# Batch 0's first attention in another order: q loaded ahead of v, and q's and a1's transposes ahead of the products with v

## The chip, the cores and the metric

The kernel runs on one core of one Trainium2 chip. The metric is the time of one execution on the device in microseconds (us). Three runs of the kernel before gave 770.55, 770.76 and 771.34 us; the median is 770.76 us.

## The reference

```python
def sm_attn(qq, kk, vv):                      # softmax attention, scale = 1/8
    s = scale * np.matmul(qq, kk.transpose(0, 1, 3, 2))
    s = s - np.max(s, axis=-1, keepdims=True)
    a = np.exp(s)
    a = a / (np.sum(a, axis=-1, keepdims=True) + 1e-09)
    return np.matmul(a, vv)
p_packed = sm_attn(p, k, v)                   # 32 packed rows attend to 576 keys
out = sm_attn(q, p_packed, p_packed)          # 576 queries attend to the 32 packed rows
...
h = x @ w_in                                  # x: (8*576, 512) from out; w_in (512, 2048)
g = np.maximum(h, 0.0) + np.log1p(np.exp(-np.abs(h)))
return (g @ w_out).astype(np.float32)         # w_out (2048, 512)
```

There are 8 batches of 8 heads, 576 rows of 64 numbers each, and 32 packed rows per head. The weights `w_in` and `w_out` arrive as 64-bit floats; everything else is 32 bits wide.

## The kernel before

**Per batch.** The heads of a batch are worked on in two groups of four (`g` = 0, 1). For each group the first attention takes these steps: k is turned by TensorE (`transposed`, tiles `psT_k`, copied by ScalarE into `T_k`); the scores of p against k (`scores1`, `ps1`) are copied to `a1`; maximum and exponential are taken (`softmax1_*`); the weights are turned (`a1_transposed`, tile `psa`, copied to `a1T`) and multiplied by v (`packed_products`, tile `psp`). VectorE scales the result (`pp`), TensorE turns it (`psx`), VectorE copies it (`pt`): `pt` is p_packed with its columns turned. For the second attention q is turned like k (`psT_q`, `T_q`), multiplied by `pt` (`scores2`, tile `ps2`), and VectorE transposes the scores into `a2` (L354), takes the softmax over packs of 32 (L362 to L374, with the exponential on ScalarE at L366) and transposes it into `aT` (L378).

**The feed-forward part.** It never forms p_packed times weights: `make_m` multiplies `pt` by `w_in` (tile `psm`) and splits it into a high and a low half (`mh`, `ml`), `weights` splits `aT` into `at_h` and `at_l`, and `gemm1` multiplies them into `ph`. A *unit* is one batch `b` and one slice `f` of 128 of the 2048 inner columns, so there are 16 units in a batch. Each unit has 12 products for `ph` (L606), the softplus on ScalarE and VectorE (`softplus`, tile `e`, L626 to L631), a split into `gh` and `gl`, and, two units later, 12 products with `w_out` into `acc` (L642). The next batch's attention is spread over the units of the batch ahead of it.

**The conversion of the weights.** `convert` brings 64-bit weights to 32 bits, in 32 items that are numbered in the order of use (item 0 and 1: `w_in`, 2 and 3: `w_out`, 4 and 5: `w_in`, and so on). Each item is loaded by SyncE (`x_i`, `x_o`, or a place in `rest`), read twice by ScalarE (`m` at L200, `r` at L204), worked on twice by VectorE (`t` at L206 and L211) and added by GpSimd (L219). A `w_out` item also has a ScalarE cast (`wo_h`, L238) and a VectorE subtraction (`wo_l`, L244). The buffers of `m`, `r`, `t` and `x` are few, so an item waits for an earlier one to be used up. All items are spread over batch 0: over its attention first, then over its units.

**What sets the order.** TensorE's order is that of the code. For the other engines a scheduler orders the instructions by its own estimates and by a priority, which is raised for batch 0's attention. Once ordered, each engine works its row strictly from front to back. SyncE's queue starts p, k (two groups), items 0 and 1, v (two groups), q (two groups), then items 2 to 5. A load waits until the load eight places ahead of it has landed; q's two loads in the profile wait for k's two. Batch 0's q lies in the columns of `w_in_sb` that are filled last.

**PSUM.** During batch 0's attention six banks go round. After it `make_m` and the turns of batch 1's k share two banks, so `psm` of the second slice waits for ScalarE's copies of `T_k`.

Of the kernel before, what the change touches and what calls it, by code (L numbers as in the profile page):

```python
# [9 lines left out]
F32 = mybir.dt.float32  # L10
# [16 lines left out]
def pack_attention_then_softplus_ffn(  # L27
# [11 lines left out]
    B, H, S, D = q.shape  # L39
    J = p.shape[2]  # L40
    DM, DFF = w_in.shape
    P = 128
    NP = 96
    SI = S // NP
    HS = SI // 2
    C = S // 2
    G = H * J // P
    HG = H // G
# [12 lines left out]
    work = ctx.enter_context(tc.tile_pool(name="work", bufs=2))  # L61
# [25 lines left out]
    def bank(nm):  # L87
        if spare:
            spare.append(spare.pop(0))
            pool, tag = spare[-1]  # L90
            return pool.tile([P, 512], F32, tag=tag, name=nm)
        return ps_m.tile([P, 512], F32, tag="m", name=nm)
# [165 lines left out]
    def transposed(nm, b, g, hh):  # L258

        src = loaded[nm, b, g]  # L260
        ps = bank(f"psT_{nm}_{b}_{g}_{hh}")
        for i in range(HS):
            nc.tensor.transpose(
                ps[:, i * NP:(i + 1) * NP],
                src[:, hh, 2 * i:2 * i + 2, :].rearrange("x s d -> x (s d)"),
                ident[:NP, :NP],
            )
        dst = work.tile([P, C], F32, tag="T", name=f"T_{nm}_{b}_{g}_{hh}", bufs=4)
        nc.scalar.copy(dst, ps[:, :C])  # L269
        return dst  # L270
# [12 lines left out]
    def products1(b, g, c, kT, ps=None):  # L283
        cols = slice(b % BG * J, (b % BG + 1) * J)
        return scores(1, b, g, c, lambda hh: pT[:, g * HG + hh, cols], kT, ps)

    def scores1(b, g, c, kT, a1):
        nc.scalar.copy(a1[:, c * C:(c + 1) * C], products1(b, g, c, kT))

    def softmax1_max(b, g, a1):  # L290
        m = small.tile([P, 1], F32, tag="m1", name=f"m1_{b}_{g}", bufs=1)
        nc.vector.reduce_max(m, a1, axis=AX.X)
        nm = small.tile([P, 1], F32, tag="nm1", name=f"nm1_{b}_{g}")
        nc.vector.tensor_scalar_mul(nm, m, -scale)
        return nm

    def softmax1_exp(b, g, a1, nm):
        z = small.tile([P, 1], F32, tag="z1", name=f"z1_{b}_{g}")
        nc.scalar.activation(a1, a1, AF.Exp, bias=nm, scale=scale, accum_out=z)
        return z  # L300

    def softmax1_sum(b, g, z):
        rs = small.tile([P, 1], F32, tag="rs", name=f"rs_{b}_{g}")
        nc.vector.tensor_scalar_add(rs, z, 1e-9)
        nc.vector.reciprocal(rs, rs)
        return rs

    def a1_transposed(b, g, c, a1, a1T):
        ps = bank(f"psa_{b}_{g}_{c}")
        for i in range(HS):  # L310
            o = c * C + i * NP
            nc.tensor.transpose(ps[:NP, i * P:(i + 1) * P], a1[:, o:o + NP], ident)  # L312
        nc.scalar.copy(
            a1T[:, c * HS:(c + 1) * HS, :].rearrange("x s j -> x (s j)"), ps[:NP, :HS * P]
        )
# [17 lines left out]
    def packed(b, g, a1T, rs):  # L333
        ps = bank(f"psp_{b}_{g}")[:, :D]
        packed_products(b, g, a1T, ps)
        return packed_scaled(b, g, ps, rs)

    def packed_transposed(b, g, pp):
        ps = bank(f"psx_{b}_{g}")
        nc.tensor.transpose(ps[:, :P], pp.rearrange("x i d -> x (i d)"), ident)  # L340
        pt = small.tile([P, P], F32, tag="pt", name=f"pt_{b}_{g}", bufs=2 * G)
        nc.vector.tensor_copy(pt, ps[:, :P])
        return pt
# [7 lines left out]
    def scores2(b, g, qT):  # L351
        a2 = work.tile([P, S], F32, tag="a2", name=f"a2_{b}_{g}", bufs=2)
        for c in range(2):
            nc.vector.transpose(a2[:, c * C:(c + 1) * C], products2(b, g, c, qT))  # L354
        return a2

    def by_pack(a2):
        return a2.rearrange("x (n j) -> x n j", j=J)

    def softmax2_exp(b, g, a2):  # L360
        m = small.tile([P, S // J, 1], F32, tag="m2", name=f"m2_{b}_{g}")
        nc.vector.reduce_max(m.rearrange("x n o -> x (n o)"), by_pack(a2), axis=AX.X)  # L362
        nc.vector.tensor_tensor(
            by_pack(a2), by_pack(a2), m.broadcast_to([P, S // J, J]), op=ALU.subtract
        )
        nc.scalar.activation(a2, a2, AF.Exp, scale=scale)  # L366

    def softmax2_div(b, g, a2):
        z = small.tile([P, S // J, 1], F32, tag="z2", name=f"z2_{b}_{g}")
        zf = z.rearrange("x n o -> x (n o)")  # L370
        nc.vector.reduce_sum(zf, by_pack(a2), axis=AX.X)
        nc.vector.tensor_scalar_add(zf, zf, 1e-9)
        nc.vector.reciprocal(zf, zf)
        nc.vector.tensor_tensor(  # L374
            by_pack(a2), by_pack(a2), z.broadcast_to([P, S // J, J]), op=ALU.mult
        )
        aT = work.tile([P, S], F32, tag="aT", name=f"aT_{b}_{g}", bufs=G)
        nc.vector.transpose(aT, a2)  # L378
        res[b]["aT"][g] = aT

    def attention_first(b):
# [71 lines left out]
        softmax2_div(b, 1, a2)  # L453
        yield

    def attention_next(b):


        a1 = [work.tile([P, S], F32, tag="a1", name=f"a1_{b}_{g}") for g in range(G)]
        if b == FIRST:  # L460
            for nm in ("k", "v"):
                for g in range(G):
                    load(nm, b, g)
                    yield
            yield
        kT = [quads("k", b, 0)]
        yield
        yield
        for c in range(2):
            scores1(b, 0, c, kT[0], a1[0])  # L470
        yield
        nm = softmax1_max(b, 0, a1[0])
        kT.append(quads("k", b, 1))
        yield
        load("q", b, 0)
        z = softmax1_exp(b, 0, a1[0], nm)
        yield
        rs = softmax1_sum(b, 0, z)
        yield
        a1T = work.tile([NP, SI, P], F32, tag="a1T", name=f"a1T_{b}_0", bufs=1)  # L480
        for c in range(2):
            a1_transposed(b, 0, c, a1[0], a1T)
            yield
        yield
        ps = [bank(f"ps1_{b}_{c}") for c in range(2)]
        packed_products(b, 0, a1T, ps[0][:, C:C + D])
        s1 = [products1(b, 1, c, kT[1], ps[c]) for c in range(2)]
        for c in range(2):
            nc.scalar.copy(a1[1][:, c * C:(c + 1) * C], s1[c])
        pp = packed_scaled(b, 0, ps[0][:, C:C + D], rs)  # L490
        yield
        load("q", b, 1)
        load("k", b + 1, 0)
        nm = softmax1_max(b, 1, a1[1])
        qT = [quads("q", b, 0)]
        yield
        z = softmax1_exp(b, 1, a1[1], nm)
        res[b]["pt"].append(packed_transposed(b, 0, pp))
        yield
        rs = softmax1_sum(b, 1, z)  # L500
        yield
        a1T = work.tile([NP, SI, P], F32, tag="a1T", name=f"a1T_{b}_1", bufs=1)
        for c in range(2):
            a1_transposed(b, 1, c, a1[1], a1T)
            yield
        load("k", b + 1, 1)
        qT.append(quads("q", b, 1))
        yield
        ps = [bank(f"ps2_{b}_{c}") for c in range(2)]
        packed_products(b, 1, a1T, ps[0][:, C:C + D])  # L510
        s2 = [products2(b, 0, c, qT[0], ps[c]) for c in range(2)]
        pp = packed_scaled(b, 1, ps[0][:, C:C + D], rs)
        a2 = work.tile([P, S], F32, tag="a2", name=f"a2_{b}_0", bufs=2)
        for c in range(2):
            nc.vector.transpose(a2[:, c * C:(c + 1) * C], s2[c])
        yield
        yield
        load("v", b + 1, 0)
        res[b]["pt"].append(packed_transposed(b, 1, pp))
        yield  # L520
        softmax2_exp(b, 0, a2)
        yield
        yield
        softmax2_div(b, 0, a2)
        yield
        a2 = scores2(b, 1, qT[1])
        yield
        softmax2_exp(b, 1, a2)
        yield
        load("v", b + 1, 1)  # L530
        yield
        softmax2_div(b, 1, a2)
        yield

    def attention(b):
        return attention_first(b) if b < FIRST else attention_next(b)
# [169 lines left out]
    pt = load_pack(0, (nc.sync, nc.scalar))  # L706
# [1 line left out]
    for g in range(G):  # L708
        load("k", 0, g)
    next(conv)  # L710
    for nm in ("v", "q"):
        for g in range(G):
            load(nm, 0, g)
    next(conv)
    res = [{"pt": [], "aT": {}, "m": {}} for _ in range(B)]
# [1 line left out]
    spare += [(ps_acc, "acc")] * NT + [(ps_m, "m")] * 2  # L717
    pack_transposed(0, pt)
    due = 0.0
    steps = attention(0)  # L720
    for st in range(NF * NT):
        with tc.high_priority(offset=FRONT):
            if next(steps, steps) is steps:
# [17 lines left out]
    for u in range(len(units) + LAG):  # L741
        if u < len(units):
            b, f = units[u]
# [7 lines left out]
            if f == NF - 1:  # L751
                if (b + 2) % BG == 0 and b + 2 < B:
                    pt = load_pack((b + 2) // BG, (nc.sync,))
# [33 lines left out]
        if u + 2 < len(units):  # L787


            nb, c = units[u + 2][0], units[u + 2][1] * P  # L790
# [31 lines left out]
```

## Time and profile before

| | us |
|---|---|
| median of three runs (lowest, highest) | 770.76 (770.55, 771.34) |
| the profiled execution, whole | 770.49 |
| its span, from the first to the last instruction | 768.7 |
| busy in it: TensorE matmul | 731.6 (95%) |
| VectorE | 529.7 (69%) |
| ScalarE | 431.8 (56%) |
| GpSimd | 98.7 (13%) |
| loads and stores | 55.97 MB, mean 73 GB/s |

The profile gives times in us from the first instruction. A row of the timeline is: start, time taken, engine, line, operation, written tile and read tiles (without numbers), shapes, count, and in brackets the idle time of the engine just before with what ended it. A `q` behind an engine's name (`SPq`) is its queue's own work, such as starting a load. In a table by windows each engine has its busy time in the window, with the number of instructions in brackets. TensorE's column of the clock is the share of its full clock that was granted.

### The profile page before, as it was taken

The page shows a single profiled execution, that of the slowest core. Times are in us where ns is not written, and L with a number is a line of the kernel's source. Part 1 is how long each engine was busy: PE and PEld are TensorE (multiplying, and loading weights), DVE is VectorE, ACT ScalarE, POOL GpSimd, SP SyncE. Part 2 cuts the span into 40 slices and gives each one's busy share as a digit, 9 for nine tenths or more (in the row PEclk, how much of TensorE's full clock was granted, in tenths as well). Part 3 has the DMA queues.
Part 4 walks back from the last instruction along what each step waited for, and adds up shares of the span by engine and source line. Part 5 has one row for each costly group of instructions (what it writes and reads, how often), then busy time and mean ns, then how long its engine had stood idle before and what let it go on. Part 6 is the DMA issues. An engine that isn't in the chain of part 4 may idle for free.

```text
span 768.7 us, 14169 instructions
## 1 busy us (share of the span) xinstructions
PE 731.6 (95%) x5360; PEld 579.9 (75%) x5360; DVE 529.7 (69%) x1092; ACT 431.8 (56%) x1057; POOL 98.7 (13%) x166
## 2 busy tenths in 40 slices
PE   6657998999999999999999999999999999999997
PEld 4445776787778877877887877878787877888886
DVE  2696879975787568665877568675777558665554
ACT  5667977655555455565555355565555364565540
POOL 1143444200000000000000000000000000000110
PEclk9957999999999999999999999999999999999999
DMA  9877655534312144033312134033311220010002
GB/s 218 233 187 172 177 151 130 123 73 71 69 32 72 30 64 93 1 94 62 63 31 70 32 63 93 1 87 62 63 32 56 44 32 1 1 55 1 1 1 69
DMA packets 149668, 55.97 MB, mean 73 GB/s; under 512 B 116320, under 2 KB 142944, under 8 KB 149600
## 3 DMA queue, kind: packets, MB, share of 16 engines
q1 hardware_dynamic: 149328, 55.00, 31.9%
q8 instruction: 42, 0.69, 0.4%
q14 instruction: 26, 0.21, 0.1%
q10 hardware_dynamic: 272, 0.07, 0.0%
HBM read 45.61 MB, written 9.44 MB: 72 GB/s over the span
## 4 chain that ended last, share of the span: by engine, by line
PE 85%; ACT 5%; DVE 5%; DMA 3%; issue 1%; POOL 1%; SPq 0%; DVEq 0%; ACTq 0%; POOLq 0%
PE acc L642 42%; PE ph L606 26%; PE acc_m L642 6%; PE psm L563 4%; PE ps L277 2%; DMA w_in_sb<-in_q 2%; PE psa L312 1%; PE ps L320 1%; DMA k<-in_k 1%; ACT e L628 1%; ACT m L200 1%; DVE e L631 1%; ACT e L626 1%; ACT e L629 1%; DVE t L206 1%
## 5 line engine op out<-in xcount | busy, mean ns | idle before, releaser
L642 PE MATMUL acc<-wo_h,gh 128*128 128x512 f32 x512 | 207.6, 405 | 0.0
L631 DVE SCALAR_TENSOR_TENSOR e<-ph,e 128x288 f32<-128x288 f32 x256 | 113.5, 453 | 133.9 <-ACT e L629 131.3
L626 ACT ACTIVATE e<-ph 128x288 f32<-128x288 f32 x256 | 102.3, 403 | 176.4 <-PE ph L606 153.9
L642 PE MATMUL acc<-wo_l,gh 128*128 128x512 f32 x512 | 201.2, 393 | 0.0
L642 PE MATMUL acc<-wo_h,gl 128*128 128x512 f32 x512 | 200.8, 392 | 0.0
L606 PE MATMUL ph<-at_h,mh 128*128 128x288 f32 x512 | 158.3, 310 | 13.2 <-ACT at_h L545 6.9
L606 PE MATMUL ph<-at_l,mh 128*128 128x288 f32 x512 | 151.7, 299 | 2.5 <-DVE at_l L546 2.5
L606 PE MATMUL ph<-at_h,ml 128*128 128x288 f32 x512 | 152.5, 298 | 0.0
L606 PEld LDWEIGHTS ph<-at_h,mh 128*128 128x128 f32 x512 | 97.6, 191 | 48.9 <-DVE gl L619 15.1
L635 POOL COPY rest<-e 128x64 f32<-128x64 f32 x128 | 53.3, 416 | 574.0 <-DVE e L631 541.2
L642 PEld LDWEIGHTS acc<-wo_h,gh 128*128 128x128 f32 x512 | 96.3, 188 | 26.9 <-issue 12.3
L642 PEld LDWEIGHTS acc<-wo_h,gl 128*128 128x128 f32 x512 | 96.3, 188 | 21.2
L628 ACT ACTIVATE e<-e 128x288 f32<-128x288 f32 (+1 forms) x240 | 108.7, 456 | 3.7
L629 ACT ACTIVATE e<-e 128x288 f32<-128x288 f32 (+1 forms) x240 | 108.6, 455 | 2.7
L642 PEld LDWEIGHTS acc<-wo_l,gh 128*128 128x128 f32 x512 | 96.5, 188 | 13.1
L606 PEld LDWEIGHTS ph<-at_l,mh 128*128 128x128 f32 x512 | 97.5, 191 | 6.0 <-DVE at_l L546 3.1
L606 PEld LDWEIGHTS ph<-at_h,ml 128*128 128x128 f32 x512 | 97.8, 191 | 0.2
L619 DVE TENSOR_TENSOR gl<-e,gh 128x512 fp32r<-128x512 f32 x128 | 87.5, 683 | 6.0
L578 ACT CAST mh<-psm 128x512 fp32r<-128x512 f32 (+1 forms) x72 | 36.3, 539 | 60.9 <-PE psm L563 60.7
L618 DVE CAST gh<-e 128x512 fp32r<-128x512 f32 x128 | 55.5, 434 | 5.9
L579 DVE TENSOR_TENSOR ml<-psm,mh 128x512 fp32r<-128x512 f32 (+1 forms) x72 | 43.0, 624 | 22.0 <-ACT mh L578 21.8
L563 PE MATMUL psm<-w_in_sb,pt 64*32 64x512 f32 (+1 forms) x576 | 41.4, 564 | 8.3 <-ACT T_k L269 4.8
(84 smaller groups left out, 698.2 us busy)
## 6 DMA issues: line engine op xcount, KB each, us to landing
v<-in_v SPq DMA_DIRECT2D x16, 576.0 KB, 5.4
x_i<-in_moe_w_in SPq DMA_DIRECT2D x28, 256.0 KB, 4.4
k<-in_k SPq DMA_DIRECT2D x48, 144.0 KB, 3.2
q<-in_q SPq DMA_DIRECT2D x48, 144.0 KB, 3.4
x_o<-in_moe_w_out SPq DMA_DIRECT2D x11, 512.0 KB, 3.7
out<-o SPq DMA_DIRECT2D x18, 256.0 KB, 2.5
rest<-in_moe_w_out SPq DMA_DIRECT2D x5, 512.0 KB, 6.0
k<-in_k SPq DMA_DIRECT2D x4, 576.0 KB, 6.0
```

The source lines that it names most:

```text
L563: nc.tensor.matmul(ps[hh * J:(hh + 1) * J, :n], res["pt"][g][o:o + D, hh * J:(hh + 1) * J], w_in_sb[o:o + D, hh, c * n:(c + 1) * n], start ...
L578: nc.scalar.copy(mh[:, cols], ps[:, :n])
L579: nc.vector.tensor_tensor(ml[:, cols], ps[:, :n], mh[:, cols].bitcast(F32), op=ALU.subtract)
L606: nc.tensor.matmul(phs[c], x, y[:, g, c * C:(c + 1) * C], start=(i == 0), stop=(i == 3 * G - 1))
L618: nc.vector.tensor_copy(hi, x)
L619: nc.vector.tensor_tensor(lo, x, hi.bitcast(F32), op=ALU.subtract)
L626: nc.scalar.activation(es[c], hv[c], AF.Abs)
L628: nc.scalar.activation(x, x, AF.Exp, scale=-1.0)
L629: nc.scalar.activation(x, x, AF.Ln, bias=1.0)
L631: nc.vector.scalar_tensor_tensor(es[c], hv[c], 0.0, es[c], op0=ALU.max, op1=ALU.add)
L635: nc.gpsimd.tensor_copy(rest[:, rest_at(b, f), r:r + REST], e[:, NT * P:])
L642: nc.tensor.matmul(acc, x[:, cs], y[:, f, :], start=(first and i == 0), stop=(last and i == 2),)
```

## The change

Batch 0 gets an attention function of its own, `attention_zero`; batch 1 keeps `attention_first`. It differs from `attention_first` in this: q's four turns of group 0 stand directly behind a1's turns of group 0, a1's turns of group 1 follow, and only then come the products with v of group 0, its turn, and those of group 1. For that `a1T` of group 1 gets a place of its own, that of `at_h`, which is not in use yet. The division of the second softmax of group 0 is written behind the turns of q of group 1. SyncE starts q's loads ahead of v's. The diff's core:

```diff
+    def attention_zero(b):
+        a1 = [work.tile([P, S], F32, tag="a1", name=f"a1_{b}_{g}") for g in range(G)]
...
+        nm = softmax1_max(b, 1, a1[1])
+        a1T = [
+            work.tile([NP, SI, P], F32, tag=t, name=f"a1T_{b}_{g}", bufs=1)
+            for g, t in enumerate(("a1T", "at_h"))
+        ]
+        for c in range(2):
+            a1_transposed(b, 0, c, a1[0], a1T[0])
+            yield
+            if c == 0:
+                z1 = softmax1_exp(b, 1, a1[1], nm)
+        qT = []
+        for hh in range(HG):
+            qT.append(transposed("q", b, 0, hh))
+            yield
+        rs1 = softmax1_sum(b, 1, z1)
+        for c in range(2):
+            a1_transposed(b, 1, c, a1[1], a1T[1])
+            yield
+        pp = packed(b, 0, a1T[0], rs0)
+        yield
+        res[b]["pt"].append(packed_transposed(b, 0, pp))
+        yield
+        pp = packed(b, 1, a1T[1], rs1)
+        yield
+        a2 = scores2(b, 0, qT)
+        yield
+        softmax2_exp(b, 0, a2)
+        res[b]["pt"].append(packed_transposed(b, 1, pp))
...
-    for nm in ("v", "q"):
+    for nm in ("q", "v"):
         for g in range(G):
             load(nm, 0, g)
...
-    steps = attention(0)
+    steps = attention_zero(0)
```

On TensorE, between a1's turns of group 0 and the scores of q's group 0 (`psT_q`: a turn of q; `psa`: a turn of a1; `psp`: products with v; `psx`: the turn of p_packed; in the names the batch comes first, then the group), before:

```order
L263 MATMUL psT_q_0_0_0_324<-ident_82,w_in_sb_87 128x96 x3
L312 MATMUL psa_0_1_0_337<-ident_82,a1_0_1_128 96x128 x3
L312 MATMUL psa_0_1_1_342<-ident_82,a1_0_1_128 96x128 x3
L340 MATMUL psx_0_0_349<-ident_82,pp_0_0_319 128x128
L263 MATMUL psT_q_0_0_1_353<-ident_82,w_in_sb_87 128x96 x3
L320 MATMUL psp_0_1_366<-v_0_1_107,a1T_0_1_336 32x64 x24
L263 MATMUL psT_q_0_0_2_394<-ident_82,w_in_sb_87 128x96 x3
L263 MATMUL psT_q_0_0_3_401<-ident_82,w_in_sb_87 128x96 x3
L277 MATMUL ps2_0_0_0_408<-T_q_0_0_0_328,pt_0_0_351 32x288
```

The same place in the changed kernel, from the last of q's four turns on:

```order
L263 MATMUL psT_q_0_0_3_318<-ident_82,w_in_sb_87 128x96 x3
L312 MATMUL psa_0_1_0_329<-ident_82,a1_0_1_128 96x128 x3
L312 MATMUL psa_0_1_1_334<-ident_82,a1_0_1_128 96x128 x3
L320 MATMUL psp_0_0_346<-v_0_0_107,a1T_0_0_268 32x64 x24
L340 MATMUL psx_0_0_374<-ident_82,pp_0_0_371 128x128
L320 MATMUL psp_0_1_379<-v_0_1_109,a1T_0_1_269 32x64 x24
L277 MATMUL ps2_0_0_0_408<-T_q_0_0_0_296,pt_0_0_376 32x288
```

Products with v of both groups now stand between the last turn and the scores; before, those of group 0 stood in front of all these rows and three of q's turns lay around those of group 1.

On VectorE, the end of the second softmax of batch 0 (`at_l` is the last thing that the first `ph` needs; `t` and `wo_l` are the conversion's), before:

```order
L206 TENSOR_SCALAR t_4_244<-m_4_240 128x512
L373 RECIPROCAL z2_0_1_488<-z2_0_1_488 128x18
L211 SCALAR_TENSOR_TENSOR t_4_244<-m_4_240,t_4_244 128x512
L374 TENSOR_TENSOR a2_0_1_470<-a2_0_1_470,z2_0_1_488 128x576
L546 TENSOR_TENSOR at_l_0_522<-aT_0_0_448,at_h_0_521 128x576
L378 STREAM_TRANSPOSE aT_0_1_493<-a2_0_1_470 128x576
L244 TENSOR_TENSOR wo_l_89<-r_3_216,wo_h_88 128x512
L206 TENSOR_SCALAR t_5_286<-m_5_282 128x512
L546 TENSOR_TENSOR at_l_0_522<-aT_0_1_493,at_h_0_521 128x576
L211 SCALAR_TENSOR_TENSOR t_5_286<-m_5_282,t_5_286 128x512
```

And now:

```order
L211 SCALAR_TENSOR_TENSOR t_3_218<-m_3_214,t_3_218 128x512
L373 RECIPROCAL z2_0_1_488<-z2_0_1_488 128x18
L615 TENSOR_TENSOR at_l_0_522<-aT_0_0_468,at_h_0_521 128x576
L374 TENSOR_TENSOR a2_0_1_470<-a2_0_1_470,z2_0_1_488 128x576
L244 TENSOR_TENSOR wo_l_89<-r_2_189,wo_h_88 128x512
L378 STREAM_TRANSPOSE aT_0_1_493<-a2_0_1_470 128x576
L206 TENSOR_SCALAR t_4_244<-m_4_240 128x512
L244 TENSOR_TENSOR wo_l_89<-r_3_216,wo_h_88 128x512
L615 TENSOR_TENSOR at_l_0_522<-aT_0_1_493,at_h_0_521 128x576
L211 SCALAR_TENSOR_TENSOR t_4_244<-m_4_240,t_4_244 128x512
L206 TENSOR_SCALAR t_5_287<-m_5_283 128x512
L211 SCALAR_TENSOR_TENSOR t_5_287<-m_5_283,t_5_287 128x512
```

The second step of item 4 and the first of item 5 moved behind the last `at_l`. At the other end of the softmax both steps of item 2, which stood ahead of the first `a2`, moved behind it.

On ScalarE, at the first unit's softplus (`e_0_0`: batch 0, slice 0), before:

```order
L545 CAST at_h_0_521<-aT_0_0_448 128x576
L200 ACTIVATE m_6_330<-rest_90 128x512
L204 ACTIVATE r_8_458<-x_i4_246 128x512
L545 CAST at_h_0_521<-aT_0_1_493 128x576
L200 ACTIVATE m_7_359<-rest_90 128x512
L626 ACTIVATE e_0_0_541<-ph_0_0_0_527 128x288
L626 ACTIVATE e_0_0_541<-ph_0_0_1_528 128x288
```

And now:

```order
L614 CAST at_h_0_521<-aT_0_1_493 128x576
L695 ACTIVATE e_0_0_541<-ph_0_0_0_527 128x288
L200 ACTIVATE m_6_306<-rest_90 128x512
L200 ACTIVATE m_7_339<-rest_90 128x512
L204 ACTIVATE r_8_451<-x_i4_246 128x512
L695 ACTIVATE e_0_0_541<-ph_0_0_1_528 128x288
```

The first reads of items 6 and 7 moved behind the first softplus instruction, which needs `ph`.

More of the change, by code (lines that the diff above doesn't have):

```diff
@@ L454, in attention_first @@
         yield
+    def attention_zero(b):
+        a1 = [work.tile([P, S], F32, tag="a1", name=f"a1_{b}_{g}") for g in range(G)]
+        kT = []
+        for hh in range(HG):
+            kT.append(transposed("k", b, 0, hh))
+            yield
+        for c in range(2):
+            scores1(b, 0, c, kT, a1[0])
+        yield
+        nm = softmax1_max(b, 0, a1[0])
+        kT = [transposed("k", b, 1, 0)]
+        yield
+        z0 = softmax1_exp(b, 0, a1[0], nm)
+        kT.append(transposed("k", b, 1, 1))
+        yield
+        rs0 = softmax1_sum(b, 0, z0)
+        for hh in range(2, HG):
+            kT.append(transposed("k", b, 1, hh))
+            yield
+        for c in range(2):
+            scores1(b, 1, c, kT, a1[1])
+        yield
[4 more added lines that the diff above has]
+        ]
+        for c in range(2):
+            a1_transposed(b, 0, c, a1[0], a1T[0])
[3 more added lines that the diff above has]
+        qT = []
+        for hh in range(HG):
+            qT.append(transposed("q", b, 0, hh))
+            yield
+        rs1 = softmax1_sum(b, 1, z1)
+        for c in range(2):
+            a1_transposed(b, 1, c, a1[1], a1T[1])
+            yield
+        pp = packed(b, 0, a1T[0], rs0)
+        yield
+        res[b]["pt"].append(packed_transposed(b, 0, pp))
+        yield
+        pp = packed(b, 1, a1T[1], rs1)
+        yield
+        a2 = scores2(b, 0, qT)
+        yield
+        softmax2_exp(b, 0, a2)
+        res[b]["pt"].append(packed_transposed(b, 1, pp))
+        yield
+        qT = [transposed("q", b, 1, 0)]
+        yield
+        qT.append(transposed("q", b, 1, 1))
+        yield
+        qT.append(transposed("q", b, 1, 2))
+        yield
+        qT.append(transposed("q", b, 1, 3))
+        yield
+        softmax2_div(b, 0, a2)
+        a2 = scores2(b, 1, qT)
+        yield
+        softmax2_exp(b, 1, a2)
+        yield
+        softmax2_div(b, 1, a2)
+        yield
     def attention_next(b):
```

## The prediction

> **What bounds the kernel now.** I read the page first, then the chain of work that ended last in order of time, then the windows, the waits and the timeline of the first 70 us. From the page, TensorE's busy tenths and its granted clock in 40 slices of 19.2 us:
>
> ```profile
> PE   6657998999999999999999999999999999999997
> PEclk9957999999999999999999999999999999999999
> ```
>
> After the first 80 us TensorE is busy nine tenths or more. What the change touches lies in the first two slices, so the question is how much earlier or later TensorE's closed work begins. The chain there:
>
> ```profile
> 6.32 13.92 DMA w_in_sb<-in_q
> ...
> 20.38 0.71 PE psT_q L263 x3
> ...
> 53.13 1.08 PE psm L563 x8
> 54.21 3.18 PE ph L606 x12
> 57.39 0.49 PE psT_k L263 x3
> ...
> 61.12 3.25 PE ph L606 x12
> 64.36 1.28 PE acc L642 x3
> 65.64 0.93 PE ps L277 x16
> ...
> 84.32 1.79 PE ph L606 x12
> ```
>
> Batch 0's q lands at 6.32 + 13.92 = 20.24 us and TensorE, which had nothing to do, starts on it at once: the wait that the change aims at. The same 12 products take 3.2 us at 54 and 61 us and 1.8 us at 84 us. Three stretches of the windows say what limits the time after that:
>
> ```profile
> 27.80:44.50 16.70, 7.29 (x55) 5.05 (x52) 15.96 (x32) 11.98 (x23) 4.11 (x3) 0.73 0.69 179
> 53.10:66.20 13.10, 10.30 (x57) 8.04 (x57) 9.28 (x17) 9.00 (x18) 5.23 (x5) 0.50 0.95 216
> 80.00:150.00 70.00, 65.75 (x544) 48.42 (x544) 61.94 (x129) 55.83 (x117) 28.62 (x28) 1.00 0.57 145
> ```
>
> The columns are TensorE's matmuls, its weight loads, VectorE, ScalarE, GpSimd, clock. From the first scores of q to the first `ph` VectorE is busy 15.96 of 16.70 us: the second softmax and the conversion share it, and TensorE waits. From 80 to 150 us TensorE is idle for only 4.25 us, so a delay brought in there finds little to hide in.
>
> **The loads.** For v's two loads (one row, both durations) and each of q's, from issue to landing:
>
> ```profile
> L127 SPq DMA_DIRECT2D v<-in_v x2: 479/540/602, 5.0 to 5.6; - x2
> DMA to landing us min/median/max: 10.6/11.4/12.3
> ...
> L127 SPq DMA_DIRECT2D w_in_sb<-in_q x1: 1594/1594/1594, 6.3 to 6.3; - x1
> DMA to landing us min/median/max: 13.9/13.9/13.9
> ...
> L127 SPq DMA_DIRECT2D w_in_sb<-in_q x1: 666/666/666, 8.8 to 8.8; - x1
> DMA to landing us min/median/max: 15.2/15.2/15.2
> ```
>
> The four places of 576 KB land at 5.0 + 10.6 = 15.6, 17.9, 20.2 and 8.8 + 15.2 = 24.0 us. Equal bytes and equal waits swap places, so I keep the times: q's groups now land at 15.6 and 17.9 us, v's at 20.2 and 24.0. The second group of v is the one that hurts. Before, the fourth place held q's second group, which nobody needed until 28 us.
>
> **TensorE up to the scores of q.**
>
> ```profile
> 20.89 1.48 PE L312 MATMUL psa<-ident,a 128*96 128x128 f32 x6
> ...
> 23.00 1.51 PE L320 MATMUL psp<-v,a1T 96*32 96x64 f32 x48
> ...
> 25.59 2.24 PE L277 MATMUL ps<-T_q,pt 64*32 64x288 f32 x16
> 26.33 0.51 PEld L277 LDWEIGHTS ps<-T_q,pt 64*32 64x32 f32 x12 [0.56 <-ACT T_q L269]
> 28.03 2.12 PE L263 MATMUL psT_q<-ident,w_in_sb 96*128 96x96 f32 x12
> ...
> 27.83 0.48 DVE L354 STREAM_TRANSPOSE a<-ps 128x288 f32<-128x288 f32 x1 [0.65 <-PE ps L277]
> 31.90 0.48 DVE L354 STREAM_TRANSPOSE a<-ps 128x288 f32<-128x288 f32 x1 [0.71 <-PE ps L277]
> ```
>
> q's four turns (2.1 us for 12 pieces) and a1's of group 1 (1.48 us) now fall between 15.9 and 19.7 us, where TensorE was idle; they cost nothing, and the cover is the wait for v. The products of group 0 run from 20.2 to 21.7 us. Those of group 1 wait for 24.0 and end at 25.5 us, and the scores of q stand right behind them on TensorE. Before, the scores took 2.24 us, of which 0.56 went on waiting for the last copies of q, so 1.68 at most; 16 such matmuls at 65.64 us in the chain took 0.93. Between these ends VectorE's first `a2` comes at 26.5 to 27.2 us in place of 27.83: a gain of 0.6 to 1.3 us, of which I take 1.0, and not the 5 us that the freed wait suggests. From there to group 1's scores the order is unchanged (turn of p_packed, 12 turns, copies), 31.90 - 27.83 = 4.1 us, so group 1 gains the same.
>
> **VectorE up to the first `ph`.**
>
> ```profile
> 30.43 0.75 DVE L363 TENSOR_TENSOR a<-a,m 128x576 f32<-128x576 f32 x1
> ...
> L206 DVE TENSOR_SCALAR t<-m 128x512 int32<-128x512 int32 x3 | 1.2, 402 | 0.0
> ```
>
> Between the first `a2` and the last `at_l` the work on VectorE is equal: item 2's two steps came in (they were done ahead of it, in idle time), one step each of items 4 and 5 went out. But the subtraction of group 0's maximum (L363, 0.75 us) now stands behind group 1's first transposition and no longer fills the wait in front of it, so that wait grows from 0.71 to about 1.4 us. The last `at_l` gains what the start gained less 0.7: between 0 and 0.6 us, 0.3 by the value taken.
>
> **The conversion loses.** Behind the last `at_l` there is now more to do: a second step of 0.6 us and a first step of 0.35. These meet GpSimd:
>
> ```profile
> 39.43 1.64 POOL L219 TENSOR_TENSOR w_in_sb<-t,r 128x512 int32<-128x512 int32 x1 [7.11 <-DVE t L211]
> 39.88 1.82 DVE L546 TENSOR_TENSOR at_l<-aT,at_h 128x576 fp32r<-128x576 f32 x1
> 43.21 0.75 DVE L546 TENSOR_TENSOR at_l<-aT,at_h 128x576 fp32r<-128x576 f32 x1
> 44.70 1.33 POOL L219 TENSOR_TENSOR w_in_sb<-t,r 128x512 int32<-128x512 int32 x1 [3.63 <-DVE t L211]
> 44.82 1.50 DVE L206 TENSOR_SCALAR t<-m 128x512 int32<-128x512 int32 x1
> ```
>
> `at_l` takes 0.75 us alone and 1.82 beside GpSimd's addition, and `t` at L206 takes 1.50 beside it where its mean over 27.8 to 44 us is 0.40: VectorE stands still until the addition is done. Before, item 4's addition was paid in front of the last `at_l` and one step of item 5 met another. Now item 3's is paid in front of it, and items 4's and 5's, 1.3 us each, both fall behind it, on the first steps of items 5 and 7. So the conversion is late by 0.95 us of work, plus 1.2 for the added standstill, less the 0 to 0.6 gained: 1.6 to 2.1 us at items 6 to 9, 1.8 by the values taken. That items 6 and 7 are first read behind `e` of the first unit costs nothing more, since VectorE gets to them only after that.
>
> **Who waits for it.** ScalarE's copies of `T_k` stand behind reads of items 8 and 9, and `psm` of the second slice waits for them:
>
> ```profile
> PE ph L606 <- ACT at_h L545: 6.9, 2, 6.4
> PE psm L563 <- ACT T_k L269: 4.8, 2, 2.8
> ...
> 43.70 0.33 SPq L156 DMA_DIRECT2D rest<-in_moe_w_out  x1
> 52.98 0.68 ACT L204 ACTIVATE r<-rest 128x512 int32<-128x512 uint32 x1
> ```
>
> The second row holds the two waits in front of 53.13 us. Before, ScalarE read item 9 twice between its two copies of `T_k`; now the read at L204 stands ahead of both copies, where it falls in a wait, so some 0.6 of the 1.6 to 2.1 us is given back and the second copy comes 1.0 to 1.5 us late. The second unit starts as late, although the first one ended up to 0.6 us early. The load of item 10 waits for ScalarE's reads of item 7 and starts some 3 us later; in the last two rows it started 9 us ahead of its first read, so it stays hidden.
>
> **The sum.** From 54 us on I carry the delay to the end, since each engine's row goes on in nearly the same order. One thing gives back. From 61.1 to 66.2 us TensorE works without a break at half clock. If the clock returns at the same time, a start 1.0 to 1.5 us later leaves as much less at half speed, and half of it, 0.5 to 0.75 us, comes back.
>
> ```profile
> 64.00:66.00 2.00, 2.00 (x13) 1.05 (x20) 0.24 (x1) 1.54 (x3) 0.00 (x0) 0.50 0.22 88
> 66.00:68.00 2.00, 2.00 (x22) 1.19 (x7) 1.43 (x3) 0.94 (x3) 0.24 (x1) 0.94 0.00 0
> ```
>
> So the ends are +0.5 us (the second unit's smallest delay with the give-back) and +2.1 (the conversion's largest without), and I take +1.0, near TensorE's own delay, for the late units are TensorE's by the third window. The profiled execution took 770.49 us in all, 0.27 less than the median of 770.76; 770.8 + 1.0 is 771.8 us. What a measurement of this kernel tells from no change is about 0.2%, or 1.5 us, so this counts as no change.
>
> The Trainium skill, "TensorE: Matmul & The Clock Gate", Part 1, says that the clock is halved after an idle window of about 3.4 us and returns after a busy one, and that the windows run freely. This trace agrees as far as it goes: TensorE's wait of 6.4 us for `at_h` is longer than such a window, and 0.50 was granted behind it until about 66 us. By that rule the return goes by the edge of a window and not by the start of the work; a window at half speed is worth 1.7 us, so the sum by the rule would be +1.5 us, the delay without the give-back, plus or minus 1.7 (an estimate from that page's 3.4 us).
>
> **Rivals.** *Slower: the conversion is the bound.* In 80 to 150 us VectorE is busy 61.94 of 70 us and waits mostly on its own row. If it stays the bound through batch 0, the conversion's whole 1.6 to 2.1 us arrives at the end and every standstill beside GpSimd adds to it: 772.4 to 772.9 us, and up to 774.2 with one more standstill of 1.3 us. Against it: TensorE is busy 65.75 of 70 us there. It decides from a delay of 1.5 us.
>
> *Faster: the clock returns early.* Of TensorE's stretches without a break, 53.1 to 57.9 us (4.8 us, the chain's rows) did not bring the clock back, 61.1 to 66.2 us did. If the moved first stretch does, the products at 61 us take about 1.5 us less (3.25 against 1.79), `acc` and the scores behind them at most half of 1.28 and 0.93 less, 1.0, in all 2.5 us: 769.3 us with the delay, 768.8 if the delay is only 0.5. For it: the stretch is nearly long enough. Against it: it is no longer than before.
>
> *Faster: v's second group lands earlier.* Four loads of 576 KB, if they followed each other evenly, would land 2.3 us apart as the first three do, and the fourth at 22.5 us. TensorE gets to it at 22.7, and every later time is 1.3 us earlier: the first `ph` up to 1.9 us early, the second unit between 0.3 early and 0.2 late, 770.5 us. That is no change too, unless the early `ph` counts in full; then 768.9 us.
>
> **Chances.** The forecast, +0.5 to +1.5 us: 0.38, its own range 771.3 to 772.3. The conversion as the bound, slower by more than 1.5 us: 0.36. The early clock: 0.12, two thirds of it faster by over 1.5 us, one third within. An earlier v: 0.14, of which 0.10 is within 1.5 us and 0.04 faster; and small reorderings later in batch 0's units, which no row prices, move 0.08 of the forecast's share to faster. So faster 0.08 + 0.04 + 0.08 = 0.20, same 0.30 + 0.04 + 0.10 = 0.44, slower 0.36. The range of 8 in 10 runs from 768.6 us (the early clock with the smallest delay, 768.8, and a little for the reorderings) to 774.2 us (the conversion as the bound with one more standstill).
>
> **What would show it.** Right: TensorE idle in front of `psp` at about 20 and at 24 us; the first `a2` near 27 us; the last `at_l` beginning at 42.6 to 43.2 us (43.21 before); the addition of item 4 behind it; `psm` of the second slice ending near 55.4 us in place of 54.2. Wrong: `psp` of group 1 starting before 23 us, `psm` ending before 54 us, or the clock back before 62 us.

## The result and the profile after

The changed kernel takes 775.51 us (median of 6 runs, 773.97 to 776.34) and the kernel before, on the same chip, 770.70 us (6 runs, 770.03 to 771.87). The ratio is 1.0061 with a 95% interval of 1.0048 to 1.0073: 4.7 us slower. I had forecast 771.8 us and a range up to 774.2. The profiled execution of the changed kernel took 774.99 us, with a span of 773.2.

TensorE's busy tenths and its granted clock, from the page of the changed kernel:

```profile
PE   6557998899999999999999999999999999999997
PEclk9558999999999999999999999999999999999999
```

Against the lines of before, the second slice went from 6 to 5, its clock from 9 to 5 (the fourth's rose from 7 to 8), and the eighth slice (135 to 155 us) from 9 to 8; behind it nothing differs. The early slices lose little, and the eighth is not where the change is. The chain that ended last, up to 65 us:

```profile
8.91 14.11 DMA v<-in_v
...
23.16 1.51 PE psp L320 x48
24.66 1.14 PE ps L277 x16
...
47.93 1.60 POOL r L219
...
61.78 2.74 PE ph L675 x12
```

The wait for q is gone and the wait for v's second group stands in its place, as forecast; it landed at 8.91 + 14.11 = 23.02 us. `psp` of group 1 comes behind it, then the scores of q. Three rows of the timeline (VectorE's first `a2`, its last `at_l`, TensorE's `psm` of the second slice) date the rest:

```profile
25.85 0.48 DVE L354 STREAM_TRANSPOSE a<-ps 128x288 f32<-128x288 f32 x1 [0.65 <-PE ps L277]
...
42.06 0.75 DVE L615 TENSOR_TENSOR at_l<-aT,at_h 128x576 fp32r<-128x576 f32 x1
...
52.43 2.12 PE L632 MATMUL psm<-w_in_sb,pt 64*32 64x256 f32 x16 [6.31 <-ACT T_k L269]
```

The first two stood at 27.83 and 43.21 us. `psm` now does the 16 products of both groups in one piece, where before 8 stood at 50.06 and 8 at 53.13 us, each behind a wait; it ends at 54.55 in place of 54.21. The same three stretches of the windows as before:

```profile
27.80:44.50 16.70, 6.71 (x46) 4.13 (x45) 15.21 (x29) 10.46 (x20) 4.05 (x3) 0.50 0.69 182
53.10:66.20 13.10, 10.11 (x61) 7.46 (x57) 10.16 (x17) 8.80 (x20) 6.11 (x6) 0.64 1.00 225
80.00:150.00 70.00, 63.71 (x508) 48.25 (x508) 58.72 (x123) 53.76 (x110) 27.52 (x27) 0.95 0.57 145
```

In the third, TensorE's busy time fell from 65.75 to 63.71 of 70 us, and its clock from 1.00 to 0.95. Where in it, the start of each unit's 12 `ph` products shows, read from the timelines (us; behind the first column the difference to the profiled execution of before; batch 0's units, the last row is batch 1's second). The columns beyond the changed kernel are runs of the next section:

```
unit    before  changed  changed  turns    changed   before    both
                         again    alone    softplus  softplus  ends
                                           first     all
0        38.94   -1.48   -2.59    +1.19    -1.30     -0.42     -0.53
1        54.14   +0.33   -0.76    +0.63    +0.50     -2.10     -2.19
3        69.68   -0.14   -1.18    +0.38    +0.55     -2.39     -2.05
8       102.24   -0.03   -1.07    +0.03    +0.68     -2.28     -1.94
12      128.35   +1.78   +0.49    +1.77    +1.32     -2.32     -1.96
13      136.37   +0.07   -1.22    -0.06    +1.32     -3.09     -2.73
14      141.17   +3.04   +1.75    +2.79    +2.52     -1.39     -2.24
15      146.71   +4.60   +3.32    +4.34    +2.42     -1.36     -2.06
1, 1    156.51   +4.45   +3.18    +4.19    +2.26     -1.50     -2.21
```

Up to unit 13 the changed kernel has lost nothing that stays: the 0.33 us of unit 1 is gone at unit 3, and the 1.78 us of unit 12 is gone at unit 13, where TensorE waited 1.65 us in the kernel before and does not wait now. Between the starts of units 13 and 15 it loses 4.5 us, and these stay to the end. What TensorE does there, in the chain of the changed kernel:

```profile
143.70 0.46 DVE e L700
...
144.21 3.15 PE ph L675 x12
147.36 3.00 PE acc L711 x12
```

and in the chain of the kernel before:

```profile
141.17 1.86 PE ph L606 x12
143.03 2.73 PE acc L642 x12
```

Unit 14's `ph` starts 3.04 us later, takes 1.29 us more and `acc` behind it 0.27: 4.6 us. The start first. `ph` has two banks; unit 14's cannot begin before VectorE has read unit 13's, which is the softplus step `e`. TensorE's wait in the changed kernel and in the kernel before, and then the changed kernel's row of VectorE up to that `e` (`t` is item 31's, the first `wo_l` item 30's and the second item 31's):

```profile
144.21 0.51 PE L675 MATMUL ph<-at_h,mh 128*128 128x288 f32 x1 [3.17 <-DVE e L700]
```

```profile
141.17 0.40 PE L606 MATMUL ph<-at_h,mh 128*128 128x288 f32 x1 [0.21 <-DVE e L631]
```

```profile
139.25 1.20 DVE L206 TENSOR_SCALAR t<-m 128x512 int32<-128x512 int32 x1
140.37 0.68 DVE L244 TENSOR_TENSOR wo_l<-r,wo_h 128x512 fp32r<-128x512 f32 x1
140.97 0.68 DVE L211 SCALAR_TENSOR_TENSOR t<-m,t 128x512 int32<-128x512 int32 x1
...
143.09 0.69 DVE L244 TENSOR_TENSOR wo_l<-r,wo_h 128x512 fp32r<-128x512 f32 x1 [0.45 <-POOL r L219]
143.70 0.81 DVE L700 SCALAR_TENSOR_TENSOR e<-ph,e 128x288 f32<-128x288 f32 x2
```

ScalarE's row for the same unit (two Abs at L695, then Exp at L697 and Ln at L698):

```profile
137.63 0.43 ACT L695 ACTIVATE e<-ph 128x288 f32<-128x288 f32 x1
138.42 0.67 ACT L200 ACTIVATE m<-x_o 128x512 f32<-128x512 f32 x1 [0.35 <-DVE t L211]
138.99 0.61 ACT L238 CAST wo_h<-t 128x512 fp32r<-128x512 f32 x1
139.50 0.68 ACT L366 ACTIVATE a<-a 128x576 f32<-128x576 f32 x1
140.09 0.39 ACT L695 ACTIVATE e<-ph 128x288 f32<-128x288 f32 x1
140.51 0.69 ACT L697 ACTIVATE e<-e 128x576 f32<-128x576 f32 x1
141.68 0.62 ACT L238 CAST wo_h<-t 128x512 fp32r<-128x512 f32 x1 [0.49 <-DVE t L211]
142.21 0.68 ACT L698 ACTIVATE e<-e 128x576 f32<-128x576 f32 x1
```

The kernel before at the same place, ScalarE and then VectorE:

```profile
138.26 0.41 ACT L626 ACTIVATE e<-ph 128x288 f32<-128x288 f32 x1 [0.31 <-PE ph L606]
138.70 0.69 ACT L628 ACTIVATE e<-e 128x576 f32<-128x576 f32 x1
139.42 0.69 ACT L629 ACTIVATE e<-e 128x576 f32<-128x576 f32 x1
```

```profile
140.67 0.45 DVE L631 SCALAR_TENSOR_TENSOR e<-ph,e 128x288 f32<-128x288 f32 x1
141.03 0.42 DVE L206 TENSOR_SCALAR t<-m 128x512 int32<-128x512 int32 x1
141.36 0.45 DVE L631 SCALAR_TENSOR_TENSOR e<-ph,e 128x288 f32<-128x288 f32 x1
141.73 0.68 DVE L211 SCALAR_TENSOR_TENSOR t<-m,t 128x512 int32<-128x512 int32 x1
```

The same instructions stand in another order. In the changed kernel three rows stand between unit 13's two Abs (the second starts at 140.09 in place of 138.26, 1.8 us later), and a cast that waits 0.49 us between Exp and Ln (1.0 us more). Ln ends 2.8 us later, at 142.89. By then VectorE stands at item 31's `wo_l`, which waits for GpSimd's addition, and gets to `e` at 143.70: 3.0 us later than before. None of these lines is in the diff; both kernels have the same code for units 8 to 15. The scheduler, which writes the rows by its own estimates, put the late ones in another order when the early code changed.

### The profile page after: what moved, and what is told of

Read it like the earlier page. It is cut to its first block, busy times and chain, and to the rows that moved or that the text cites. A ratio compares the mean times of both kernels' runs of the same rounds, so it can differ in the third digit from the quotient of the medians.

```text
span 773.2 us, 14179 instructions
## 1 busy us (share of the span) xinstructions
PE 732.1 (95%) x5360; PEld 581.0 (75%) x5360; DVE 531.1 (69%) x1092; ACT 432.2 (56%) x1057; POOL 97.5 (13%) x166
## 4 chain that ended last, share of the span: by engine, by line
PE 82%; DVE 7%; ACT 4%; DMA 4%; issue 2%; POOL 1%; SPq 0%; DVEq 0%; ACTq 0%; POOLq 0%
PE acc L711 41%; PE ph L675 26%; PE acc_m L711 6%; PE psm L632 4%; PE ps L277 2%; DMA v<-in_v 2%; PE ps L320 1%; DVE t L211 1%; DMA x_o<-in_moe_w_out 1%; PE psa L312 1%; DVE e L700 1%; DMA k<-in_k 1%; DVE t L206 1%; DVE wo_l L244 1%; ACT m L200 1%
## 5 line engine op out<-in xcount | busy, mean ns | idle before, releaser
L695 ACT ACTIVATE e<-ph 128x288 f32<-128x288 f32 x256 | 102.1, 403 | 179.6 <-PE ph L675 158.9
L697 ACT ACTIVATE e<-e 128x288 f32<-128x288 f32 (+1 forms) x240 | 108.6, 456 | 3.7
L698 ACT ACTIVATE e<-e 128x288 f32<-128x288 f32 (+1 forms) x240 | 108.5, 455 | 2.6
```

The costliest lines, as they stand in the source:

```text
L695: nc.scalar.activation(es[c], hv[c], AF.Abs)
L697: nc.scalar.activation(x, x, AF.Exp, scale=-1.0)
L698: nc.scalar.activation(x, x, AF.Ln, bias=1.0)
```

## The experiments

Theory: those late rows make the loss. Rivals: the new loads or the new turns cost by themselves, or the early conversion's delay is carried. "Changed" below is the changed kernel, "before" the kernel before; ratios are to before on the same chip, whose medians were 769.6 to 770.3 us in these runs.

**The changed kernel again** (changed_again), unedited.

> The changed kernel itself, unedited, timed beside the other three. Theory (the loss is in the rows and so belongs to the program): ratio to the kernel before 1.005 to 1.007, with the PE wait of 3.0 to 3.4 us ahead of unit 14. Rival (a chance of the first profile, such as a late transfer): the wait is elsewhere or under 2 us.

Ratio 1.0070 (1.0055 to 1.0085). TensorE's wait ahead of unit 14 is the same to 0.01 us:

```profile
142.92 0.57 PE L675 MATMUL ph<-at_h,mh 128*128 128x288 f32 x1 [3.16 <-DVE e L700]
```

In the table this execution is 1.0 to 1.3 us ahead of the first one at every unit from the first on. So much varies from one execution to the next, and it is carried; the wait is the same in both.

**The turns alone** (turns_alone). `for nm in ("v", "q")` as before, with `attention_zero`.

> The changed kernel with v loaded ahead of q again, so the new turns stand without the new loads. The rows of units 12 to 15 come out word for word as in the changed kernel. Theory (late rows): 774.5 to 776 us, with the PE wait of about 3.2 us ahead of unit 14, though the first q turns come later here. Rival one (the loads' order costs, since v's transfers end later): 770 to 771.5 us. Rival two (the early change carries its delay): no wait at unit 14, and the loss stands at units 0 to 3.

773.84 us, 0.7 below the times that I expected, ratio 1.0060 (1.0048 to 1.0072). Its late rows are those of the changed kernel, and so is its wait:

```profile
143.96 0.40 PE L675 MATMUL ph<-at_h,mh 128*128 128x288 f32 x1 [3.02 <-DVE e L700]
```

The order of the loads is not needed for the loss. Its first units start between 0.5 us early and 1.2 us late, and unit 8 starts 0.03 us late: no early delay is left to be carried.

**The loads alone** (loads_alone). q ahead of v, with `attention_first`.

> The kernel before with q loaded ahead of v and its old turns. Its late rows are a third version: t_31 and wo_l_31 stand ahead of unit 13's e on VectorE, but t_30 and wo_l_30 further ahead, and unit 13's e ahead of a2's exponential on ScalarE. Theory (late rows): a part of the loss, 771.5 to 775 us, with a PE wait ahead of unit 14 between 0.5 and 3.5 us that equals the loss to 1.5 us. Rival (loads cost by v's later landing, carried to the end): the loss stands already at unit 1 and no wait is at unit 14.

771.39 us, ratio 1.0024 (1.0013 to 1.0035), with the wait between the others':

```profile
141.38 0.40 PE L675 MATMUL ph<-at_h,mh 128*128 128x288 f32 x1 [1.25 <-DVE e L700]
```

Its units 3 to 8 started 1.0 to 1.5 us earlier than before's, and that was gone again at units 9 (+0.2 us) and 14 (+0.2). That the load order is worth something early is not shown by this: before_softplus_first, a run below whose rows are those of the kernel before up to unit 8, stood 1.3 us earlier at units 3 to 8 too, with a clock of 0.77 from 62 to 66 us in place of 0.50.

**The changed kernel with the late rows of before** (after_softplus_first; in the table "changed softplus first"). The first softplus step of units 8 to 15 of batch 0 gets a higher priority:

```diff
-            next(chain)
+            if b == 0 and f >= 8:
+                with tc.high_priority(offset=30):
+                    next(chain)
+            else:
+                next(chain)
```

> The changed kernel, early rows untouched; the first softplus step of batch 0's units 8 to 15 gets a higher priority of 30. That gives the rows of units 12 and 13 the very order of the kernel before: t_31 between unit 13's two e, wo_l_31 behind them, m_31 and r_31 behind unit 13's three ScalarE rows. Theory (late rows make most of the loss, the early part a smaller rest of up to 1.7 us that is carried): ratio to the kernel before 1.000 to 1.002, no PE wait over 0.8 us at unit 14, and units 3 to 10 between 0 and 1 us later than before. Rival (the early change makes the loss): ratio 1.005 to 1.007.

770.56 us, ratio 1.0000 (0.9990 to 1.0010). The loss is gone, with loads and turns as changed. No wait is left at unit 14; TensorE waits at unit 13 for item 29, as it did before (the second line):

```profile
137.09 0.67 PE L632 MATMUL psm<-w_in_sb,pt 64*32 64x256 f32 x16 [1.66 <-POOL w_in_sb L219]
```

```profile
135.77 0.67 PE L563 MATMUL psm<-w_in_sb,pt 64*32 64x256 f32 x16 [1.65 <-POOL w_in_sb L219]
```

(Its profiled execution took 772.74 us, the highest of its 11 runs, so its column in the table lies some 2 us above its median. The 1.2 us between units 13 and 14 are a clock of 0.50 from 138.25 to 141.60 us, behind that wait; behind the same wait the execution of before kept the full clock.) The control, before_softplus_first, is the same edit in the kernel before.

> The control: the same priority in the kernel before, where it moves few rows (unit 8's e ahead of wo_l_22, unit 14's e ahead of a2's division). Theory: ratio 0.998 to 1.0005, so that what the other run gains is not a gain that the priority gives any kernel. Rival (the priority is itself a gain of some 3 us): ratio 0.996.

769.85 us, ratio 0.9991 (0.9980 to 1.0002): the priority by itself is worth some 0.1%, which the interval does not tell from nothing, and not the 0.6 to 0.7% that it gives back to the changed kernel. From unit 9 to 240 us its rows of ScalarE, VectorE and GpSimd are those of after_softplus_first but for one copy (`mh`), so the two differ by the early change. The changed kernel is 0.7 us longer here, and the 11 times of each run spread over some 3 us; neither nothing nor the 1.0 us that I had forecast is excluded.

**Two other ways to move the late rows.** First (after_rows_freed), unit 13's softplus step and the conversion's steps from unit 12 on (a higher priority for the one, a lower one for the others):

```diff
+            if (b, f) == (0, 13):
+                with tc.high_priority(offset=60):
+                    next(chain)
...
+                        if f >= 12:
+                            with tc.high_priority(offset=-60):
+                                next(conv, None)
```

> The changed kernel with its early rows as they are. Only the rows of batch 0's last units move: the conversion's steps of units 12 to 15 get a lower priority and unit 13's first softplus step a higher one, so that on VectorE t_31 and wo_l_31 stand behind unit 13's e, as they do in the kernel before. Theory (the loss is made by the rows at units 13 and 14: 3.2 us of PE wait and 1.3 us of half clock after it): the 4.5 us come back, 770.5 to 771.5 us, ratio to the kernel before 1.000 +- 0.001, and PE no longer waits 3.17 us ahead of unit 14. Rival (the early change itself costs: q ahead of v, or the later conversion, and the delay is carried to the end): 774.5 to 775.5 us, as the changed kernel.

771.33 us, ratio 1.0022 (1.0012 to 1.0031): 3 of 4.7 us came back, less than I had expected. The wait fell as expected:

```profile
142.19 0.40 PE L675 MATMUL ph<-at_h,mh 128*128 128x288 f32 x1 [0.62 <-DVE e L700]
```

Where the other 1.7 us lie is open. This edit leaves the rows of units 8 to 12, which the one above changes; but in its profiled execution, which ends 0.9 us after that of before, 0.8 us stood at unit 8 already and 0.6 at unit 13. Second (after_one_step), unit 13's step alone:

> The changed kernel with a higher priority for unit 13's first softplus step alone. t_31 and wo_l_30 stay ahead of unit 13's e on VectorE, and r_31 and m_31 on ScalarE; wo_l_31 goes behind the e, and the second Abs, Exp and Ln go ahead of a2's exponential and of the two wo_h casts. Theory (the wait of 3.17 us is the sum of the rows that stand ahead): the wait falls to 0.5 to 1.5 us and with it the half clock behind it, ratio 1.002 to 1.0035. Rival (only VectorE's t_31 rows beside GpSimd's adds count): the wait stays over 2.5 us, ratio 1.005 to 1.006.

773.30 us, ratio 1.0035 (1.0022 to 1.0048). Some four tenths came back, the upper end of the ratio that I expected; the wait is longer than the 0.5 to 1.5 us expected:

```profile
142.78 0.40 PE L675 MATMUL ph<-at_h,mh 128*128 128x288 f32 x1 [2.02 <-DVE e L700]
```

With `wo_l` of item 31 behind `e` and Ln ahead of the second cast, the wait lost 1.15 us (one cast still stood ahead of Exp, and the attention's exponential ahead of Ln), and unit 14's products ran at full clock. So waits of 3.17, 2.02 and 0.62 us go with ratios of 1.006 to 1.007, 1.0035 and 1.0022.

**Late rows alone, in the kernel before** (before_late_rows). Nothing ahead of unit 10 is changed:

```diff
-                        next(conv, None)
+                        if (f, t) >= (10, 2):
+                            with tc.high_priority(offset=200):
+                                next(conv, None)
+                        else:
+                            next(conv, None)
```

> The kernel before, with nothing changed ahead of unit 10: v is loaded first, attention's turns stand as they stood. Only the conversion's steps from unit 10's third output tile on get a higher priority, and that puts t_31 and wo_l_31 ahead of unit 13's e on VectorE, and m_31 and r_31 ahead of it on ScalarE, as the changed kernel has them (here a2's division stands there too). Theory (the late rows alone make the loss): 774 to 776.5 us, ratio 1.004 to 1.008, with a PE wait of 3 to 5 us ahead of unit 14. Rival (the early change makes it): 770.7 us, ratio 1.000.

773.90 us, ratio 1.0061 (1.0046 to 1.0076). The ratio is as expected; the wait is mostly another one:

```profile
138.85 0.67 PE L563 MATMUL psm<-w_in_sb,pt 64*32 64x256 f32 x16 [3.31 <-POOL w_in_sb L219]
...
146.69 0.40 PE L606 MATMUL ph<-at_h,mh 128*128 128x288 f32 x1 [1.08 <-DVE e L631]
```

The edit also put item 29's steps behind unit 12's `gh` and `gl`, so its addition came 1.7 us later than the rows around it and `psm` of the last slice waited for it. It shows that rows alone, with no early change, cost as much; that it is by the very wait of the changed kernel it does not show. In this execution k's second load took 1.5 us longer than in the profiled one of before. Every row ahead of unit 10 is the same, and its units were 1.53 us late at unit 0 and 1.42 at unit 12: a pure delay was carried.

**Is an early gain kept?** Softplus first in all of batch 0's units (`b == 0`), in the kernel before (before_softplus_all):

> The kernel before with the same priority for all of batch 0's units. Its order comes out with t_31 and wo_l_30 ahead of unit 13's e on VectorE, and r_31 ahead of its second exponential on ScalarE; so the theory expects a PE wait of 1 to 3 us ahead of unit 14 and a loss there, though softplus has the priority and though the loads and attention's turns are the old ones: ratio 1.001 to 1.005. Rival (softplus first is better everywhere): 0.995 to 0.999.

769.13 us, ratio 0.9982 (0.9971 to 0.9993): faster, where I had expected a loss. The wait at unit 14 was there as expected:

```profile
139.78 0.40 PE L606 MATMUL ph<-at_h,mh 128*128 128x288 f32 x1 [1.89 <-DVE e L631]
```

I had left out what the rows of units 0 to 3 would give: the second unit starts 2.1 us earlier, and 1.7 of it is gained behind the first unit, as in the next two runs. At unit 14, 1.7 us of what stood at unit 13 is lost. Two runs, both_ends and both_ends_late, keep that edit and change only the rows from unit 13 on, by a priority for the conversion that is lower by 10 or by 60 from `f >= 12` on.

> The kernel before with the priority for all of batch 0's softplus steps, as in before_softplus_all, and a lower priority of 10 for the conversion's steps from unit 12 on. Rows differ from before_softplus_all at units 13 and 14 alone: t_31's second pass goes between unit 13's two e and wo_l_30 behind them on VectorE, and the last Ln ahead of wo_h's cast on ScalarE. Theory (an early gain is carried to the end where no row stops it; the 1.7 us that before_softplus_all lost between units 13 and 14 were its rows): the PE wait of 1.89 us at unit 14 falls under 0.9 us, and the ratio to the kernel before is 0.9955 to 0.998, some 1 us under before_softplus_all. Rival (the conversion's own data bind at unit 14, whatever the rows): the wait stays and the ratio is 0.998 to 0.9995.

> As both_ends, with a lower priority of 60 for the conversion from unit 12 on: t_31's second pass, wo_l_30 and wo_l_31 go behind unit 13's e, a2's division and aT altogether, up to unit 14's e. Theory: no wait over 0.9 us at unit 14, ratio 0.9955 to 0.998; the last casts are then 3 us later than in both_ends, and nothing waits for them before unit 15's output tiles. Rival (the late wo_l holds up the output tiles of unit 15 or the attention of batch 1): 0.998 to 1.002 with a wait behind unit 14.

768.17 us, ratio 0.9975 (0.9965 to 0.9986), and 768.91 us, 0.9977 (0.9966 to 0.9988). The waits at unit 14:

```profile
138.93 0.40 PE L606 MATMUL ph<-at_h,mh 128*128 128x288 f32 x1 [0.69 <-DVE e L631]
```

```profile
138.50 0.40 PE L606 MATMUL ph<-at_h,mh 128*128 128x288 f32 x1 [0.85 <-DVE e L631]
```

They fell by 1.2 and 1.0 us, and unit 14 stands 1.2 and 1.05 us better against before_softplus_all than unit 13 does; the gain reaches the end. The conversion's data do not bind there. Both beat the kernel before and the changed one, by 0.2 to 0.25% and by 0.8 to 0.95%. Between the two and before_softplus_all the intervals overlap.

**With the changed loads.** Three more runs put softplus first where q is loaded ahead of v: from unit 8 on with the old turns, and in all units with the old and with the new turns.

> The kernel before with q loaded ahead of v alone (old turns) and the higher priority for units 8 to 15. With the loads alone units 3 to 8 came 1.0 to 1.5 us earlier, and that was lost again at units 9, 10 and 14, where conversion rows stand ahead of softplus rows. Theory (the rows decide what of an early gain is kept): ratio 0.997 to 0.9995, faster than before. Rival (the gain is lost anyway, by the conversion's data): ratio 1.001 to 1.0035.

> q loaded ahead of v, old turns, and the priority for all of batch 0's units; the late rows stand as in the kernel before. With the priority from unit 8 on the ratio was 0.9996. Theory: 0.997 to 1.0005, since the conversion sets the early units and the late rows cost nothing here. Rival (rows of units 0 to 7 that hold the conversion back cost later): 1.001 to 1.004.

> The changed kernel with the higher priority for the first softplus step of all of batch 0's units, so that rows move in units 0 to 7 too. Unit 13's e stands ahead of wo_l_31 and beside t_31, as in the kernel before. Theory (what unit 14 waits for decides): ratio 0.998 to 1.002, no PE wait over 1 us at unit 14. Rival (the new turns cost 4 us wherever the late rows stand): 1.004 to 1.007.

Ratios 0.9996 (0.9986 to 1.0005), 1.0000 (0.9989 to 1.0011) and 0.9993 (0.9983 to 1.0004). The gain that I expected of the first is not shown, and its late rows are not those of before: item 31's steps stand ahead of unit 13's `e`, and TensorE waits 1.09 us for an `e` ahead of unit 12. The other two have the late rows of before_softplus_first, and with these the new loads, and loads and turns together, give nothing that the runs can tell.

## Why the prediction was wrong

**The early steps held.** TensorE waited for v's second group, q's and a1's turns fell into idle time, VectorE's first `a2` came 2.0 us earlier and the conversion later. What was off was one landing: I took 24.0 us for v's second group and it came at 23.02. That 1.0 us runs through all later steps: last `at_l` at 42.06 against 42.6 to 43.2 forecast, conversion 0.9 us late against 1.6 to 2.1 (GpSimd's addition of item 6, in the chain's row at 47.93 us, stood at 47.06 in before's), second unit 0.33 us late against 1.0 to 1.5. The rival of an earlier v (landing 22.5 us, second unit between 0.3 early and 0.2 late) came nearest; its time was 770.5 us, and it has no term for what came later.

**The clock.** I had put 61 us as a place where the clock could return early. It returned for one window and went again, as two rows of the windows of the changed kernel show (clock in the third column from the end):

```profile
59.00:62.30 3.30, 0.52 (x4) 0.53 (x5) 2.06 (x5) 3.01 (x6) 1.80 (x2) 1.00 1.12 215
62.40:65.70 3.30, 3.30 (x13) 2.58 (x11) 2.51 (x4) 1.50 (x3) 1.03 (x2) 0.50 0.84 229
```

The products at 61.78 us took 2.74 us in place of 3.25, so the give-back was 0.5 us, of the size that I had named and for another reason. The clock back before 62 us was one of my signs of being wrong, and it came; it did not make the loss.

**The step that failed** is "From 54 us on I carry the delay to the end, since each engine's row goes on in nearly the same order". The carrying is right where all engines are late or early together: 1.5 us of k were carried to unit 12, and the gain of both_ends to the end. A delay of TensorE alone need not be: the 1.78 us of unit 12 were gone at unit 13. "In nearly the same order" is wrong. I had followed each row up to the first units and took the rest for granted, though the rows at unit 13 were there to be compared. The term that was mis-sized is "small reorderings later in batch 0's units, which no row prices": I gave it 0.08, all of it to faster. Measured, one such reordering is 3.0 us of wait and 1.6 us of half clock. With the priority that gives it before's late rows, the change came out at 1.0000 (0.9990 to 1.0010), 770.7 us on the scale of the forecast of 771.8, and 0.7 us above the control with the same priority. Whether the sum of the early terms held by itself these times cannot tell.

**The slower rival** (the conversion is the bound, up to 774.2 us) named the right engine rows and the wrong mechanism. The conversion does stand in front of softplus at unit 13, but by its place in the rows and not by its work: it is the same work in both kernels, and putting softplus ahead of it gives the time back.

## What to carry to other kernels

Where a scheduler orders the rows, an edit at one place can change the rows at every other: compare the rows of both kernels to the end, and look for rows that have slipped between the steps which free a buffer that the bounding engine waits for. To learn what the edit itself is worth, hold the late rows fixed by a priority and give the kernel before the same priority as a control. A priority for the steps that free the bounding engine's buffers was worth more here than the change (0.9982 with before's loads, and 0.9975 and 0.9977 with the conversion's last steps put lower as well).

## What the runs showed of the hardware

A wait of 3.17 us cost 1.6 us more by the clock. Windows of the changed kernel around unit 14:

```profile
141.00:144.20 3.20, 0.04 (x1) 0.00 (x0) 2.75 (x7) 1.40 (x3) 1.27 (x1) 1.00 0.31 63
144.40:147.60 3.20, 3.20 (x14) 3.10 (x14) 3.20 (x8) 0.62 (x2) 0.24 (x1) 0.50 0.89 209
147.70:150.00 2.30, 2.30 (x12) 1.85 (x10) 0.73 (x2) 1.48 (x3) 0.00 (x0) 0.99 1.21 213
```

The idle stretch itself shows the full clock, the busy one behind it half, and 3.4 us later it is full again: `ph` took 3.15 in place of 1.86 us. I had also not expected that TensorE need not be idle throughout:

```profile
120.40:123.80 3.40, 1.65 (x19) 0.79 (x20) 3.40 (x8) 2.23 (x5) 1.98 (x2) 1.00 0.49 126
123.85:127.15 3.30, 3.30 (x14) 3.01 (x13) 2.68 (x6) 2.11 (x5) 1.28 (x1) 0.50 0.38 96
```

TensorE was busy for 1.65 of 3.40 us, and half clock followed. In after_one_step a wait of 2.02 us was followed by the full clock. TensorE's busy share alone does not decide: in turns_alone it was busy for 2.00 of 3.35 us from 121.20 us on and 0.50 followed, in the kernel before for 1.87 of 3.35 us from 73.00 us on and 1.00 followed. Nor does the wait: 1.65 us ahead of unit 13 left the clock of before at 1.00, and 1.66 us at the same place in after_softplus_first was followed by 0.50.

The Trainium skill, "TensorE: Matmul & The Clock Gate", Part 1, gives free-running windows of about 3.4 us, a half clock after an idle one and a full clock after a busy one. The lengths here agree with it; the rows at 120.40 us show that a window that is half busy can count as idle, and where the bound lies no run here shows. One stretch does not fit: from 24.90 to 28.25 us of the changed kernel TensorE's records are busy throughout, with turns and narrow products, and the clock from 28.30 to 31.60 us is still 0.50.
